# Seven block products for one more pair of batches in a fused attention and two-layer feed-forward kernel, with a new table of order and buffers

## Chip, core and metric

The kernel runs on one core of a Trainium2 chip. The metric is the device time of one execution in microseconds. The core has five engines with a queue of instructions each: TensorE (PE) multiplies matrices into the eight banks of its accumulation memory, VectorE (DVE), ScalarE (ACT) and GpSimd (POOL) do elementwise work, and SyncE (SP) issues the transfers between main memory and on-chip memory. GpSimd works here on on-chip tiles alone, never on a bank.

## The reference, cut to what matters

```python
def _attn_ref(x, state):                      # x 4 x 8 x 512 x 64, state 4 x 8 x 32 x 64
    scores = scale * np.matmul(x, state.transpose(0, 1, 3, 2))
    ...
    xread = np.matmul(softmax(scores), state)
    scores2 = scale * np.matmul(state, x.transpose(0, 1, 3, 2))
    ...
    sread = np.matmul(softmax(scores2), x)
    return np.concatenate([xread, sread], axis=2)

def _moe_ref(x, w_in, w_out):                 # first layer, 2176 tokens, 512 -> 2048 -> 512
    h = x @ w_in
    g = np.maximum(h, 0.0) + np.log1p(np.exp(-np.abs(h)))
    return g @ w_out

def _moe2_ref(x, w_gate, w_val, w_out):       # second layer, 512 -> 1536 -> 512
    g = x @ w_gate
    silu = g * (1.0 / (1.0 + np.exp(-g)))
    return silu * (x @ w_val) @ w_out
```

The attention's result is the input of the first layer, and that layer's result the input of the second.

## The kernel before

Every operand of a large product is split into a high part, rounded to the type fp32r, and a low part, the remainder. A product then is three matmuls: high by high, weight-low by high, weight-high by low (`THREE`).

The first layer's 2048 hidden columns are worked in four chunks `c` of 512, each chunk in four blocks `ft` of 128 columns, and the tokens in four batches `b` of 512. A unit is (c, b, ft) and has the number n = 16c + 4b + ft. The step `p<n>` (function `p1`, L758) makes the unit's hidden block in a bank from the attention weights and the product of state and input weights: six matmuls of 512 columns. `sp<n>` (class `Softplus`) takes the softplus on ScalarE, and `gl<n>` (`g_low`) the low part. The steps `mm`, `mh`, `ml` make the products of state and input weights (L710) and split them; `s1`, `s1h`, `s1l`, `s3`, `s4` carry the 128 state rows through the same layer.

The product with `w_out` goes two ways. For a pair (c, q) of batches 2q, 2q+1 that is not in the set `SEVEN`, each unit has a step `P<n>` (`p2`, L782): its hidden block by the four column blocks of `w_out` into four banks, 12 matmuls, summed over `ft`. After four of them `y_add` moves the banks to the tile `y`. For a pair in `SEVEN`, the two batches and the two halves of `ft` are a 2 by 2 matrix of blocks B11, B12 (batch 2q+1, first half), B21 (batch 2q, second half), B22, and the product with the 2 by 2 matrix of `w_out` is made with seven block products instead of eight: `y_part` (L896) in the order P1, P2, P5, P3, P6, P7, P4, as steps `P<16c+8q>` and on. Each has 12 matmuls in two banks. They need sums of blocks, T1 = B12 - B11, T3 = B22 - B12, T2 = T3 + B11, T4 = B21 - T2 (`g_sum`, L865, steps `g.T1<c><q><f>`), split again (`gh`, L870; `gL`, L877), and sums of the weights (`ws.<c><i>`, L833; `wsh`, L837; `wsl`, L841). P1, P6, P7 and P4 share a pair of banks, and so do P2, P5 and P3; behind each step two additions (`ya`, `yb`, function `y_put`, L796 to L800) bring the banks to `y`.

The second layer (`q1` to `q7`, L1011; `om` L1048; `op` L1072) follows the same scheme, with weights that were split early, stored to main memory and loaded again (`lg<n>`, `lw<n>`, `ls<q>`).

The order of all work is a table of names written out by hand or by a planner, `ORDER`: the kernel calls the steps in that order, each engine executes its instructions in it, and an exclamation mark behind a name moves an elementwise step from its usual engine to the other of VectorE and GpSimd. A second table, `HOMES`, says which bank or buffer holds each tile. Steps `warm` are small matmuls of constants that fill TensorE's time at the start; there are 39 in both kernels.

```python
    SEVEN = {(1, 0), (1, 1), (2, 0), (2, 1), (3, 0), (3, 1)}
    SEQUENCE = ("P1", "P2", "P5", "P3", "P6", "P7", "P4", None)
```

## Time and profile before

| | us |
|---|---|
| median of 3 runs | 711.68 (711.34 to 711.95) |
| the profiled execution | 711.46 |
| its span, first to last record | 709.7 |
| TensorE busy | 701.7 |
| VectorE busy | 567.0 |
| ScalarE busy | 400.7 |
| GpSimd busy | 160.5 |

The span is what the trace covers; the execution's own time has some 1.8 us around it. Busy times count overlapping records of one engine once. The records of matmuls overlap, since one begins before the end of the one ahead.

### The profile page before, as it was taken

How to read it: one execution, taken by the hardware profiler on the slowest of the kernel's cores; microseconds unless marked ns; L12 is line 12 of the kernel's file. 1: busy time of each engine (PE TensorE's matmuls, PEld its weight loads, DVE VectorE, ACT ScalarE, POOL GpSimd, SP SyncE). 2: the span in 40 equal slices, each digit the busy share in tenths (PEclk: the TensorE clock that was granted, in tenths of full speed). 3: DMA queues.
4: the chain of work that ended last, by engine and by line, in shares of the span. 5: the costliest groups of instructions: out<-in, count | busy, mean ns of one | idle time of the engine just before them, and what ended most of it. 6: DMA issues, size and time to landing. Idle time of an engine off the chain costs nothing.

```text
span 709.7 us, 10357 instructions
## 1 busy us (share of the span) xinstructions
PE 701.7 (99%) x3696; PEld 563.8 (79%) x3696; DVE 567.0 (80%) x967; ACT 400.7 (56%) x740; POOL 160.5 (23%) x149
## 2 busy tenths in 40 slices
PE   8999999999999999999999999999999999999997
PEld 5687878786877778888888888888888888887886
DVE  4986545799999999899677788778886988777686
ACT  4987566666775766558665647645552434334231
POOL 0343223325342404250302110013050000122000
PEclk9999999999999999999999999999999999999999
DMA  8980002044142420465867387565969899777603
GB/s 329 397 327 1 1 1 89 31 167 160 54 126 89 149 90 2 142 229 160 271 219 253 121 297 261 184 240 188 357 237 327 299 297 335 265 283 260 249 0 120
DMA packets 48628, 134.90 MB, mean 190 GB/s; under 512 B 5440, under 2 KB 17728, under 8 KB 48576
## 3 DMA queue, kind: packets, MB, share of 16 engines
q1 hardware_dynamic: 48576, 134.24, 53.1%
q8 instruction: 29, 0.48, 0.3%
q14 instruction: 23, 0.19, 0.1%
HBM read 93.06 MB, written 41.16 MB: 189 GB/s over the span
## 4 chain that ended last, share of the span: by engine, by line
PE 97%; DVE 2%; POOL 1%; ACT 0%; issue 0%; ACTq 0%; DVEq 0%
PE b L1011 32%; PE b L896 16%; PE b L758 12%; PE b L1048 11%; PE b L1072 7%; PE b L782 6%; PE b L1096 2%; PE b L710 2%; PE b L954 2%; PE b L974 2%; PE b L1334 1%; PE b L1129 1%; PE b L601 1%; POOL d L833 0%; PE b L681 0%; POOL d L766 0%
## 5 line engine op out<-in xcount | busy, mean ns | idle before, releaser
L1011 PE MATMUL b<-k,k 128*128 128x512 f32 x1008 | 242.6, 390 | 0.0
L1011 PEld LDWEIGHTS b<-k,k 128*128 128x128 f32 x1008 | 187.9, 188 | 39.9 <-ACT d L1270 0.5
L896 PE MATMUL b<-d,k 128*128 128x512 f32 x366 | 98.0, 393 | 0.2
L758 PE MATMUL b<-k,k 128*128 128x512 f32 x384 | 94.9, 392 | 0.0
L1253 DVE TENSOR_TENSOR d<-b,d 128x512 f32<-128x512 f32 x96 | 64.7, 685 | 31.5 <-PE b L1011 23.7
L1270 ACT ACTIVATE d<-b 128x512 f32<-128x512 f32 x72 | 42.5, 592 | 82.9 <-PE b L1011 69.8
L758 PEld LDWEIGHTS b<-k,k 128*128 128x128 f32 x384 | 71.3, 188 | 19.6 <-issue 3.4
L1036 DVE TENSOR_TENSOR k<-b,k 128x512 f32<-128x512 f32 x110 | 73.5, 684 | 16.4 <-PE b L1072 9.1
L896 PEld LDWEIGHTS b<-d,k 128*128 128x128 f32 x366 | 67.7, 188 | 20.0 <-issue 1.0
L1048 PE MATMUL b<-d,k 128*128 128x512 f32 x308 | 77.8, 390 | 0.0
L1048 PEld LDWEIGHTS b<-d,k 128*128 128x128 f32 x308 | 57.5, 188 | 11.8
L800 DVE TENSOR_TENSOR k<-b,k 128x512 f32<-128x512 f32 x84 | 56.4, 684 | 9.6 <-PE b L896 9.2
L421 DVE SCALAR_TENSOR_TENSOR d<-d,k 128x512 int32<-128x512 int32 x65 | 44.8, 696 | 11.9 <-ACT k L415 11.9
L1072 PE MATMUL b<-d,k 128*128 128x512 f32 x202 | 51.7, 391 | 0.0
L1017 ACT ACTIVATE d<-d 128x512 fp32r<-128x512 f32 x58 | 35.4, 626 | 27.0 <-DVE d L1253 11.5
L415 ACT ACTIVATE k<-k 128x512 int32<-128x512 uint32 x68 | 44.9, 669 | 0.0
L1072 PEld LDWEIGHTS b<-d,k 128*128 128x128 f32 x202 | 37.7, 188 | 8.4 <-DVE d L1024 0.5
L766 POOL TENSOR_TENSOR d<-d,d 128x512 fp32r<-128x512 f32 x22 | 30.0, 1367 | 63.3 <-ACT d L745 46.3
L1024 DVE TENSOR_TENSOR d<-d,d 128x512 fp32r<-128x512 f32 x48 | 35.0, 735 | 9.4 <-ACT d L1017 8.3
L896 PE MATMUL b<-k,k 128*128 128x512 f32 x138 | 42.2, 393 | 0.0
L782 PE MATMUL b<-d,k 128*128 128x512 f32 x160 | 39.7, 391 | 0.0
L740 ACT ACTIVATE d<-b 128x512 fp32r<-128x512 f32 x40 | 23.8, 596 | 23.7 <-PE b L758 13.4
(193 smaller groups left out, 1064.4 us busy)
## 6 DMA issues: line engine op xcount, KB each, us to landing
k<-gv_d SPq DMA_DIRECT2D x60, 512.0 KB, 6.9
gv_d<-k SPq DMA_DIRECT2D x48, 512.0 KB, 4.1
k<-in_moe_w_out_dram SPq DMA_DIRECT2D x28, 512.0 KB, 5.6
k<-w_d SPq DMA_DIRECT2D x23, 512.0 KB, 8.1
k<-in_moe_w_in_dram SPq DMA_DIRECT2D x16, 512.0 KB, 7.8
k<-in_moe_w_gate_dram SPq DMA_DIRECT2D x48, 128.0 KB, 3.8
k<-in_moe_w_val_dram SPq DMA_DIRECT2D x48, 128.0 KB, 3.6
w_d<-k SPq DMA_DIRECT2D x12, 512.0 KB, 4.2
```

What stands on the lines that cost most here:

```text
L415: nc.scalar.activation(self.bot, low_word, AF.Copy, bias=-0.5 + 7.5 * 2.0 ** -18, scale=2.0 ** -29 * (1 - 2.0 ** -18),)
L421: nc.vector.scalar_tensor_tensor(out=ti, in0=ti, scalar=3, in1=self.bot, op0=ALU.logical_shift_left, op1=ALU.bitwise_or,)
L758: nc.tensor.matmul(ps, halves[s3], others[t3], start=par == 0 and n3 == 0, stop=par == NPAR - 1 and n3 == 2)
L782: nc.tensor.matmul(yps[c, b, dt], halves[s3], t[t3], start=ft == 0 and n3 == 0, stop=ft == FT - 1 and n3 == 2)
L800: nc.vector.tensor_tensor(out=v, in0=ps, in1=v, op=ALU.add)
L896: nc.tensor.matmul(ps, halves[s3], g[t3], start=part in OPENS and f == 0 and n3 == 0, stop=f == 1 and n3 == 2, skip_group_check=True)
L1011: nc.tensor.matmul(ps, halves[s3], others[t3], start=first and i == 0 and n3 == 0, stop=i == 1 and n3 == 2, skip_group_check=True)
L1036: nc.vector.tensor_tensor(out=v, in0=ps, in1=v, op=ALU.add)
L1048: nc.tensor.matmul(ps, halves[s3], act[n + f, j][t3], start=f == 0 and n3 == 0, stop=f == 1 and n3 == 2)
L1072: nc.tensor.matmul(ps, halves[s3], act[n, t][t3], start=opens and n3 == 0, stop=n3 == 2, skip_group_check=True)
L1253: eng.tensor_tensor(out=o(), in0=x(), in1=y(), op=op)
L1270: op(f"{name}.{n}", lambda n=n, k=k: nc.scalar.activation(fresh(n, k), cs[n]["x"], AF.Copy))
```

## The change

The pair (0, 1), batches 2 and 3 of the first chunk, is made with seven block products. `ORDER` and `HOMES` are rewritten as a whole: the order of every engine changes. In the class that makes the weight sums of the second layer's output, a branch is added for groups q with 2q in `SEVEN2` = {12, 14, 16, 18, 20}; the groups that the kernel makes have q from 0 to 5.

```diff
-    SEVEN = {(1, 0), (1, 1), (2, 0), (2, 1), (3, 0), (3, 1)}
+    SEVEN = {(0, 1), (1, 0), (1, 1), (2, 0), (2, 1), (3, 0), (3, 1)}
...
+            self.now = 2 * q in SEVEN2
...
+                if self.now:
+                    self.raw.append(w2[2 * q + f])
+                    continue
...
+            if self.now:
+                w2s[self.q, k] = o
```

Of the table, the lines around the step P10 after the change, with the one around P10 before, and the lines with the load `lg18` in both:

```diff
-    "al7! hd.w11 p12 hd.w12 s1l.0 hd.w13 P10 tl.w11 tl.o12 tl.w12 p13 P11 sp13 ya11 tl.w13 yb11 sp12 mm.11 ab.o13",
+    "tl.o12 P9 sp12 g.T1011 s1l.0 yb8 hd.w12 gh.T1011 g.T1010 tl.w12 p14 gh.T1010 yb9 gL.T1010! mm.11 sp14",
+    "gL.T1011! ya9 P10 mh.111 g.T3010 ab.o11 ml.111 g.T2010 gh.T3010 g.T4010 gh.T2010 mm.10 ab.o13 gL.T2010! mh.110",
...
-    "op.14P2 lg18 oa.12P40 c1.16 as.16 oa.14P10 th.14B22 oa.12P41 q4.16 th.14T1 os.h31 tL.14T1! op.14P5 oa.14P20",
+    "op.14P5 os.l31! tL.14T2! q6.17 lg18 b2.16 bs.16 op.14P6 th.16B11 b1.17 q5.17 tL.14T3! oa.14P50 q7.17 oa.14P51",
```

TensorE's queue late in the second pair of the first chunk, before: the step P14 (L782, four banks, a weight block d and the hidden block k) and the first-layer step p16 (L758).

```order
L782 MATMUL b_74<-d_882,k_408 128x512 x2
L782 MATMUL b_74<-d_654,k_408 128x512
L782 MATMUL b_75<-d_882,k_408 128x512 x2
L782 MATMUL b_75<-d_654,k_408 128x512
L782 MATMUL b_70<-d_882,k_408 128x512 x2
L782 MATMUL b_70<-d_654,k_408 128x512
L782 MATMUL b_69<-d_882,k_408 128x512 x2
L782 MATMUL b_69<-d_654,k_408 128x512
L758 MATMUL b_72<-k_470,k_818 128x512 x3
L758 MATMUL b_72<-k_390,k_1020 128x512 x3
```

TensorE's queue at the same place after the change, where the lines are numbered 13 higher: two first-layer steps, p19 and p17 (L771), and P13 (L909), a block step on T3 in two banks.

```order
L771 MATMUL b_69<-k_470,k_1036 128x512 x3
L771 MATMUL b_69<-k_394,k_465 128x512 x3
L771 MATMUL b_75<-k_470,k_1036 128x512 x3
L771 MATMUL b_75<-k_394,k_465 128x512 x3
L909 MATMUL b_70<-d_582,k_706 128x512 x2
L909 MATMUL b_70<-d_559,k_706 128x512
L909 MATMUL b_70<-d_1080,k_580 128x512 x2
L909 MATMUL b_70<-k_1083,k_580 128x512
L909 MATMUL b_73<-d_582,k_706 128x512 x2
L909 MATMUL b_73<-d_559,k_706 128x512
L909 MATMUL b_73<-d_1080,k_580 128x512 x2
L909 MATMUL b_73<-k_1083,k_580 128x512
```

A step of 12 matmuls stays one of 12, in two banks instead of four; there is one such step fewer in the pair, and its operands are weights and block sums.

VectorE's queue between the low parts of the state rows (L965) of the first and the second chunk, before: 12 instructions, pieces of weights (L421, L428), low parts of products with the state (L718) and copies to y (L798).

```order
L421 SCALAR_TENSOR_TENSOR d_356<-d_356,k_117 128x512
L428 SCALAR_TENSOR_TENSOR d_220<-k_107,d_220 128x512
L428 SCALAR_TENSOR_TENSOR d_299<-k_105,d_299 128x512
L428 SCALAR_TENSOR_TENSOR d_256<-k_115,d_256 128x512
L798 COPY k_107<-b_73 128x512
L428 SCALAR_TENSOR_TENSOR d_356<-k_117,d_356 128x512
L718 TENSOR_TENSOR k_997<-b_76,k_997 128x512
L798 COPY k_117<-b_75 128x512
```

VectorE's queue between the same two instructions (L978) after the change, a part of the 44 that stand there: the sums of the second block row (L878), their low parts (L890), a low part from a bank (L777) and a copy and an addition to y (L811, L813).

```order
L878 TENSOR_TENSOR d_245<-b_74,d_245 128x512
L878 TENSOR_TENSOR d_141<-d_245,d_141 128x512
L878 TENSOR_TENSOR d_182<-d_182,d_141 128x512
L890 TENSOR_TENSOR k_1066<-d_141,k_826 128x512
L890 TENSOR_TENSOR k_1083<-d_245,d_1080 128x512
L890 TENSOR_TENSOR k_1088<-d_182,d_1085 128x512
L777 TENSOR_TENSOR d_1096<-b_74,d_1057 128x512
L731 TENSOR_TENSOR k_465<-b_76,k_465 128x512
L811 COPY k_576<-b_75 128x512
L428 SCALAR_TENSOR_TENSOR d_314<-d_314,k_109 128x512
L813 TENSOR_TENSOR k_576<-b_70,k_576 128x512
```

The sums and low parts of the new pair stand in one row on VectorE between work on weights that was there before.

## Rows read from the trace of the kernel before

**Rows 1.** Page, busy us (share of the span) and instructions of each engine.

```profile
PE 701.7 (99%) x3696; PEld 563.8 (79%) x3696; DVE 567.0 (80%) x967; ACT 400.7 (56%) x740; POOL 160.5 (23%) x149
```

**Rows 2.** Page, the chain that ended last, share of each engine.

```profile
PE 97%; DVE 2%; POOL 1%; ACT 0%; issue 0%; ACTq 0%; DVEq 0%
```

**Rows 3.** Waits of TensorE: releaser, us in total, times, longest.

```profile
PE b L669 <- ACT d L614: 2.2, 3, 1.1
PE b L1334 <- DVE ones L372: 1.1, 1, 1.1
PE b L1334 <- ACT d L614: 0.4, 1, 0.4
PE b L1334 <- DVE k L718: 0.2, 1, 0.2
```

**Rows 4.** Stretches: length, busy PE, PEld, DVE, ACT, POOL, then granted clock, transfers.

```profile
0.00:17.70 17.70, 14.99 (x106) 9.85 (x106) 8.04 (x20) 7.94 (x16) 1.75 (x7) 1.00 0.88 328
17.70:35.50 17.80, 16.59 (x315) 10.67 (x312) 17.32 (x38) 16.86 (x39) 6.88 (x6) 1.00 1.02 398
35.50:86.20 50.70, 50.70 (x314) 41.33 (x313) 34.27 (x59) 38.14 (x70) 18.38 (x13) 1.00 0.29 115
86.20:122.10 35.90, 35.90 (x208) 27.70 (x207) 19.75 (x33) 21.48 (x41) 10.31 (x10) 1.00 0.14 45
122.10:333.40 211.30, 211.09 (x1066) 165.86 (x1065) 192.11 (x318) 143.27 (x262) 67.81 (x61) 1.00 0.33 111
333.40:692.00 358.60, 358.60 (x1639) 297.33 (x1638) 283.39 (x486) 170.61 (x311) 55.31 (x53) 1.00 0.70 248
```

**Rows 5.** Timeline 59 to 104 us, in parts: start, us covered, instructions merged.

```profile
59.65 0.39 PE L782 MATMUL b<-d,k 128*128 128x512 f32 x1
...
86.62 1.89 DVE L428 SCALAR_TENSOR_TENSOR d<-k,d 128x512 int32<-128x512 int32 x3
90.28 2.88 PE L782 MATMUL b<-d,k 128*128 128x512 f32 x12
...
93.09 1.09 PE L710 MATMUL b<-d,d 64*32 64x512 f32 x16
...
97.29 1.09 ACT L714 ACTIVATE k<-b 128x512 fp32r<-128x512 f32 x2
...
98.21 3.73 PE L954 MATMUL b<-d,d 128*128 128x128 f32 x32
```

**Rows 6.** Groups by line and shape: busy us, mean ns, idle before.

```profile
L865 DVE TENSOR_TENSOR d<-b,d 128x512 f32<-128x512 f32 x20 | 13.5, 684 | 1.7 <-ACT d L745 0.8 <-ACT b L742 0.5 <-POOL k L437 0.3
L833 DVE TENSOR_TENSOR d<-d,d 128x256 f32<-128x256 f32 x7 | 2.9, 420 | 0.1
L877 POOL TENSOR_TENSOR d<-d,k 128x512 fp32r<-128x512 f32 x3 | 3.9, 1300 | 30.2 <-PE b L896 21.8 <-ACT k L870 8.4
L870 ACT ACTIVATE d<-d 128x512 fp32r<-128x512 f32 x32 | 19.7, 626 | 20.6 <-PE b L896 12.8 <-DVE d L865 5.6 <-POOL d L865 1.3
L742 ACT ACTIVATE b<-b 128x512 f32<-128x512 f32 x24 | 14.3, 596 | 2.3 <-PE b L758 2.2
```

**Rows 7.** Timeline 122 to 140 us, first pair of the second chunk.

```profile
122.08 3.30 PE L896 MATMUL b<-d,k 128*128 128x512 f32 x12
122.83 2.14 PEld L896 LDWEIGHTS b<-d,k 128*128 128x128 f32 x10 [0.55 <-POOL d L766]
...
136.14 1.42 PE L896 MATMUL b<-d,k 128*128 128x512 f32 x5
...
139.38 0.84 PE L974 MATMUL b<-k,k 128*128 128x512 f32 x3
```

**Rows 8.** Loads of the second layer's split gate and value weights (L520), issue to landing.

```profile
DMA to landing us min/median/max: 3.9/6.9/11.4
```

**Rows 9.** Timeline at P0 and at the last addition.

```profile
41.33 2.91 PE L782 MATMUL b<-d,k 128*128 128x512 f32 x12
...
705.83 0.69 DVE L1036 TENSOR_TENSOR k<-b,k 128x512 f32<-128x512 f32 x1 [0.67 <-PE b L1048]
```

540 rows, old and new, of tables (HOMES, ORDER) are left out of this document.

## Prediction

> **What bounds the kernel now.** First I read the page's busy times: TensorE (PE) is busy 99% of the span (709.7 us), VectorE (DVE) 80% and ScalarE (ACT) less [rows 1]. The chain of work that ended last then says whether that share is the path: 97% of it is TensorE's [rows 2]. Third, the list of waits on TensorE names everything that it waited for: 3.9 us in all, and each releaser belongs to the first layer's attention or to the start (L614 is the exponential of the scores, L372 the first constant) [rows 3]. Fourth, busy times by stretch: TensorE lacks 2.7 us of the first 17.7 us and 1.2 us of the next 17.8, and from then on only 0.2 us until 692 us [rows 4]. So behind the start the reader is to see one engine that never stands still for long: a matmul taken out there shortens the run by its own pitch, if the work in front of the next matmul is ready.
>
> A busy TensorE can hide short waits, since its records overlap. So I also looked at the pitch: twelve second-layer matmuls of the first chunk (L782) that follow each other cover 2.88 us, one record alone 0.39, so eleven steps take 2.49 us, or 0.226 us each [rows 5]. Such blocks are the ones that the change touches, and they run without a pause. The granted clock is 1.00 throughout, the level of 2.4 GHz [rows 4].
>
> **What the change removes.** In the first chunk, batches 2 and 3 have eight steps P8 to P15 of 12 matmuls of 512 columns each. After the change there are seven, P8 to P14, of 12 each (two banks, two blocks, three products). No other group of matmuls changes in number; the filler matmuls are the same 39. So 12 x 0.226 = **2.72 us** leave TensorE, in a stretch where it is 100% busy.
>
> The Trainium skill ("TensorE: Matmul & The Clock Gate", "Back-to-back issue gap") gives about 131 ns as the sustained pitch of such matmuls with weight loads between them. By it twelve would be worth an estimated 1.57 us. This trace has 0.226 us for this very line, and the measurement decides, so I give the page's figure no chance.
>
> **What it adds.** By the table and the functions: 8 block sums (L865), 8 roundings (L870), 8 low parts (L877), 2 weight sums of four half-width instructions (L833) with 4 roundings and 4 low parts, and 6 more additions into the y tile (L800), while 2 low parts of the first layer fall away. As the lists of instructions count it, VectorE gets 16 more, GpSimd 16, ScalarE 12. One costs 0.68 us on VectorE (0.42 half wide), 1.30 on GpSimd, 0.63 on ScalarE [rows 6]. All of this would be some 10 us of VectorE, put at nothing on the path because TensorE runs meanwhile: from P8 to P16 VectorE was busy 19.75 of 35.90 us [rows 4].
>
> Is that cover enough? In the table from P8 to P16 I count 38 full-width and 4 half-width VectorE instructions before, 57 and 8 after. In line, three full-width ones take 1.89 us, so the pitch is (1.89 - 0.69) / 2 = 0.60 us [rows 5]. Then 57 x 0.60 + 8 x 0.42 = 37.6 us. TensorE has there seven block steps of 2.72, ten first-layer steps of 6 x 0.226 = 1.36, three score products of about 1.25 (1.09 for the row and its start), and one state product of 3.7 us [rows 5]: 19.0 + 13.6 + 3.75 + 3.7 = 40.1 us. So 2.5 us of VectorE stay free; without the overlap of neighbours (0.684 each [rows 6]) it would need 39.0 + 3.4 = 42.4 us, 2.3 too many. Which applies? From 122 to 333 us VectorE ran 318 instructions in 211.3 us and TensorE lacked 0.2 us [rows 4]; that stretch keeps its number of VectorE instructions in the table to within 16 short ones. I take the pitch.
>
> **Hand-offs in the new pair.** A block step can't start before its operand is summed, rounded and has its low part. The tightest that I find is P10, on T1 = B12 - B11. Behind p12 TensorE has P9, p14 and one score product, 2.72 + 1.36 + 1.25 = 5.3 us. VectorE has nine instructions from T1's first sum to its last low part, 5.4 us by the pitch, and may begin some 0.6 us before p12 ends, because p13, 1.36 us earlier, feeds the first (a softplus of 0.60 lies between): it ends at 4.9, 0.4 us ahead. Such margins can fail. The same hand-off exists in the first pair of the next chunk: there the first block step took 3.30 us for its twelve instead of 2.88, a loss of 0.42, its weight loads having waited for GpSimd's low part [rows 7]; the step P18 took 139.38 - 136.14 = 3.24 us to the next group instead of 2.72, a loss of 0.52. So the new pair costs between 0 and 0.94 us more; I take the one of the opening step, **0.42 us**, as its margins are of the size of these losses.
>
> **The order of the rest.** All other instructions are reordered. Up to P0 both tables have the same TensorE steps, and the waits there come to 2.8 us apart from the first constant [rows 3]: that much could go at most. Ahead of P0, which starts at 41.3 us [rows 9], stand one more full VectorE step and two more ScalarE steps in the table, 0.60 + 2 x 0.49 = 1.6 us if nothing hides them (two ScalarE instructions in line cover 1.09 us [rows 5], one about 0.60). I put the start at no change, ends -2.8 and +1.6. The tail keeps its shape: VectorE's last addition starts at 705.83 us and a store follows [rows 9].
>
> **Sum.** The profiled execution took 711.46 us: its span of 709.7 and 1.8 around it. 711.46 - 2.72 + 0.42 = **709.2 us**. The median of the runs, 711.68, stands 0.2 above the profiled one, which I leave inside the range.
>
> **The rivals.**
> The start gets longer (0.10): attention's exponentials already hold TensorE up there, and more steps now stand in front; against it, TensorE needs nothing of these extra steps before P0. 711.46 - 2.72 + 1.6 = 710.3 us; 710.8 with the hand-off.
>
> VectorE becomes the bound from P8 to P16 (0.12): for it, 0.684 us is what one instruction occupies, and the stretch goes from half full to nearly full; against it, the pitch of neighbours is 0.60, and fuller stretches passed without a wait. 711.46 - 2.72 + 2.3 = 711.0 us: the gain is nearly eaten. The Trainium skill ("Perfetto Trace Analysis", "Identifying the Most-Contended Engine") takes occupancy as the fair measure for Vector and not for matmuls; weight loads at 79% would stand level with VectorE's 80% here, and by that rule it is this rival that comes true.
>
> A late weight load makes it slower (0.06): the place is the load lg18 ahead of the step q1.18 in the second half. Before, 11 TensorE steps of 1.36 us stand between them in the table, 15.0 us; after, four (op.14P6, q5.17, q7.17, op.14P3), 5.4 us. Loads of this kind land after 3.9 to 11.4 us, 6.9 in the median [rows 8]. SyncE's queue issues in order, so later loads move with it. At the median the wait is 1.5 us, time 710.7; at the longest 6.0 us, time 709.2 + 6.0 = 715.2. From a landing of 9.4 us it is slower by over 0.2%. Against it: TensorE waited for no such load before [rows 3], leads of 6.8 us (lg13, lg16) among them, and the first product needs only the first of four tiles.
>
> The start gets shorter (0.05): its longest single wait of 1.1 us goes [rows 3], 711.46 - 2.72 - 1.1 = 707.6 us. The edit in the weight sums of the second half changes nothing: its condition asks for 2q among 12 to 20, and q goes to 5.
>
> **How the numbers follow.** The likeliest case, TensorE shorter by its twelve matmuls and hand-offs of 0 to 0.94 us, holds 0.67: 708.7 to 709.7, forecast 709.2. 0.2% of 711.46 is 1.42 us, about what a measurement of this kernel can tell from no change; so faster is below 710.0, slower above 712.9. Faster: 0.67 and 0.05, and of the start-up and VectorE cases, which need not reach their full price, 0.07: 0.79. Slower: the late load from 9.4 us on, 0.04. The rest, 0.17, is the same. The range for 8 in 10 reaches from the shorter start, 707.6, to the VectorE bound, 711.0; it leaves out the longer loads and, at the low end, a start without any wait.
>
> **What the profile after would show.** TensorE 12 matmuls fewer (3684), busy 2 to 3 us less, its busy time still 99%, and no wait over 0.3 us by the list behind 40 us: then the first term is right. In the new pair, block steps that cover over 2.9 us show the hand-off's price; two of them at 0.4 or more put the sum too low. VectorE over 95% busy in the stretch around P8 to P16 with TensorE's weight loads waiting for VectorE would be the second rival; a wait of TensorE on a load of gv_d behind 500 us the third. The prediction is wrong if P0 starts more than 1 us from its place before, 41.3 us, or if the stretch behind P16 loses more than it did.

## Result and the profile after

The changed kernel takes 716.29 us in the median (715.55 to 716.44, 4 runs) against 711.51 of the kernel before (711.32 to 711.95, 4 runs): ratio 1.0064, 95% interval 1.0047 to 1.0082. It is slower by 4.8 us where 2.3 us less were forecast. Executions of one kernel with and without a fall of TensorE's clock (below) stand together in a median. Lines below carry the changed kernel's numbers: 7 above those of before up to L531 (before's L421 is L428, its L428 is L435, its L437 is L444), 13 above from L583 on.

The page of the profiled execution (716.37 us, span 714.6), busy us by engine, to be held against [rows 1]: TensorE has its 12 matmuls fewer and is busy 1.0 us *longer*.

```profile
PE 702.7 (98%) x3684; PEld 561.2 (79%) x3684; DVE 584.0 (82%) x983; ACT 408.4 (57%) x752; POOL 178.7 (25%) x165
```

Waits of TensorE after (releaser, us in total, times, longest), beside [rows 3]. The longest one on the exponential (L627, before's L614) has grown from 1.1 to 1.9 us, and four kinds of 0.5 us and more are new: L795 on GpSimd, L707 on ScalarE, L771 on VectorE, L1024 on a transfer.

```profile
PE b L682 <- ACT d L627: 2.8, 2, 1.9
PE b L1347 <- DVE ones L379: 1.0, 1, 1.0
PE b L795 <- POOL d L779: 0.9, 1, 0.9
PE b L707 <- ACT d L703: 0.9, 2, 0.4
PE b L771 <- DVE d L777: 0.8, 1, 0.8
PE b L1024 <- DMA k<-gv_d: 0.5, 2, 0.3
```

To see where the time went, both spans are cut at the same steps: P0, P8, P16 (stretch, length, busy PE, PEld, DVE, ACT, POOL, granted clock, transfers). First before, at 41.33, 79.27 and 122.08:

```profile
0.00:41.33 41.33, 37.41 (x503) 25.39 (x504) 29.86 (x65) 30.27 (x65) 11.11 (x15) 1.00 0.96 369
41.33:79.27 37.94, 37.94 (x196) 30.74 (x195) 25.36 (x43) 28.67 (x53) 13.47 (x11) 1.00 0.24 91
79.27:122.08 42.81, 42.81 (x239) 33.41 (x238) 24.14 (x40) 25.47 (x48) 12.72 (x12) 1.00 0.12 38
122.08:709.70 587.62, 583.50 (x2763) 474.29 (x2761) 487.68 (x822) 316.32 (x576) 123.14 (x114) 1.00 0.55 195
```

The same of the changed kernel:

```profile
0.00:43.90 43.90, 38.10 (x503) 25.34 (x504) 31.00 (x66) 30.64 (x65) 11.90 (x16) 0.96 0.89 334
43.90:83.45 39.55, 38.63 (x196) 30.58 (x195) 33.01 (x55) 30.37 (x57) 14.83 (x12) 1.00 0.19 76
83.45:124.76 41.31, 40.51 (x228) 30.93 (x227) 35.33 (x60) 28.87 (x53) 6.14 (x5) 1.00 0.14 39
124.76:714.60 589.84, 585.49 (x2763) 474.37 (x2761) 484.64 (x805) 318.55 (x579) 145.84 (x134) 1.00 0.56 196
```

TensorE's counts agree in every stretch but the pair's (3696 and 3684 in all). The start is 2.57 us longer, P0 to P8 1.61 longer, the changed pair 1.50 *shorter*, the rest 2.22 longer: +4.90 in all. So the place that the edit names did gain, though 1.2 us less than its matmuls, and three places that the forecast put at no change lost 6.4.

What TensorE and its releasers do at those places, from the timeline after (start, us covered, engine, line, instructions merged, the idle time before):

```profile
10.74 0.63 PE L682 MATMUL b<-ident,d 128*128 128x128 f32 x4 [1.92 <-ACT d L627]
...
12.03 1.96 PE L614 MATMUL b<-k,d 64*32 64x512 f32 x16
...
25.58 1.36 POOL L664 TENSOR_TENSOR d<-d,r 128x512 f32<-128x512 f32 x1 [6.51 <-DVE r L660]
25.96 0.67 DVE L643 TENSOR_REDUCE m<-d 128x16 f32<-128x512 f32 x1
...
27.91 1.04 POOL L664 TENSOR_TENSOR d<-d,r 128x512 f32<-128x512 f32 x1
28.00 1.50 DVE L428 SCALAR_TENSOR_TENSOR d<-d,k 128x512 int32<-128x512 int32 x1 [0.32 <-ACT k L422]
28.60 2.04 PE L723 MATMUL b<-d,d 64*32 64x512 f32 x16
...
48.29 1.88 PE L795 MATMUL b<-d,k 128*128 128x512 f32 x7 [0.92 <-POOL d L779]
...
97.72 0.69 DVE L890 TENSOR_TENSOR d<-d,d 128x512 fp32r<-128x512 f32 x1 [0.60 <-ACT d L883]
98.33 0.68 DVE L777 TENSOR_TENSOR d<-b,d 128x512 fp32r<-128x512 f32 x1
99.07 1.66 PE L771 MATMUL b<-k,k 128*128 128x512 f32 x6 [0.80 <-DVE d L777]
...
134.37 1.58 PE L723 MATMUL b<-d,d 64*32 64x512 f32 x16
...
616.21 6.14 SPq L583 DMA_DIRECT2D k<-w2s_d  x2
622.47 1.98 SPq L527 DMA_DIRECT2D k<-gv_d  x4
629.03 0.94 PE L1024 MATMUL b<-k,k 128*128 128x512 f32 x3 [0.21 <-DMA k<-gv_d]
```

Four readings. TensorE stands 1.92 us ahead of the first transposes (L682), and a score product behind them (L614) takes 1.96 us for its sixteen matmuls where before it took 1.09. A product of state and weights at 28.60 takes 2.04 us against 1.09 [rows 5]: one of its weight blocks comes from L428, which lasts 1.50 us there. At 99.07 the first-layer step p15 waits until VectorE has read its bank (L777); that step of VectorE stands behind a low part (L890) which waited 0.60 us for ScalarE's rounding (L883). At 629 a product waits for a load (L527, lg20) that stood in SyncE's queue behind a load of weight sums (L583), which itself waited 6 us for a buffer.

The granted clock belongs to the first reading. The stretches after: at 11.37, behind the idle time, it drops to 0.50 (1.2 GHz) for 3.4 us.

```profile
0.00:11.37 11.37, 8.18 (x54) 6.28 (x55) 2.67 (x7) 2.06 (x3) 0.70 (x6) 1.00 0.81 276
11.37:14.79 3.42, 3.42 (x24) 1.53 (x24) 1.63 (x4) 2.34 (x5) 1.05 (x1) 0.50 1.03 418
```

### The profile page after: what moved, and what is told of

Its sections match the earlier page's. It is cut to its first block, busy times and chain, and to the rows that moved or that the text cites. A ratio compares the mean times of both kernels' runs of the same rounds, so it can differ in the third digit from the quotient of the medians.

```text
span 714.6 us, 10385 instructions
## 1 busy us (share of the span) xinstructions
PE 702.7 (98%) x3684; PEld 561.2 (79%) x3684; DVE 584.0 (82%) x983; ACT 408.4 (57%) x752; POOL 178.7 (25%) x165
## 4 chain that ended last, share of the span: by engine, by line
PE 92%; DVE 3%; DMA 3%; POOL 1%; issue 1%; ACT 1%; SPq 0%; ACTq 0%; POOLq 0%
PE b L1024 30%; PE b L909 19%; PE b L771 13%; PE b L1061 11%; PE b L1085 6%; PE b L795 3%; PE b L1109 2%; PE b L723 2%; PE b L967 2%; PE b L987 2%; PE b L1142 1%; DMA k<-gv_d 1%; DMA k<-in_xt_dram 1%; DMA w2s_d<-k 1%; PE b L1347 1%
## 5 line engine op out<-in xcount | busy, mean ns | idle before, releaser
L1024 PE MATMUL b<-k,k 128*128 128x512 f32 x1008 | 243.5, 391 | 0.5 <-DMA k<-gv_d 0.5
L1024 PEld LDWEIGHTS b<-k,k 128*128 128x128 f32 x1008 | 187.6, 188 | 40.4 <-DVE k L1049 0.8
L909 PE MATMUL b<-d,k 128*128 128x512 f32 x576 | 141.1, 394 | 0.0
L909 PEld LDWEIGHTS b<-d,k 128*128 128x128 f32 x576 | 106.4, 188 | 30.8 <-issue 2.5
L771 PE MATMUL b<-k,k 128*128 128x512 f32 x384 | 94.7, 393 | 0.8 <-DVE d L777 0.8
L1049 DVE TENSOR_TENSOR k<-b,k 128x512 f32<-128x512 f32 x110 | 73.0, 685 | 21.3 <-PE b L1085 12.7
L771 PEld LDWEIGHTS b<-k,k 128*128 128x128 f32 x384 | 71.2, 188 | 20.7 <-DVE d L777 1.7
L1061 PE MATMUL b<-d,k 128*128 128x512 f32 x336 | 82.8, 390 | 0.0
L779 POOL TENSOR_TENSOR d<-d,d 128x512 fp32r<-128x512 f32 x35 | 48.9, 1410 | 113.7 <-ACT d L758 54.1
L1061 PEld LDWEIGHTS b<-d,k 128*128 128x128 f32 x336 | 63.0, 188 | 13.6 <-DVE d L1037 0.3
L1030 ACT ACTIVATE d<-d 128x512 fp32r<-128x512 f32 x63 | 38.9, 627 | 43.8 <-DVE d L1266 25.2
L813 DVE TENSOR_TENSOR k<-b,k 128x512 f32<-128x512 f32 x90 | 60.5, 684 | 3.6 <-PE b L909 3.0
L428 DVE SCALAR_TENSOR_TENSOR d<-d,k 128x512 int32<-128x512 int32 x67 | 48.9, 739 | 10.1 <-ACT k L422 9.9
L1085 PE MATMUL b<-d,k 128*128 128x512 f32 x210 | 53.3, 392 | 0.0
L883 ACT ACTIVATE d<-d 128x512 fp32r<-128x512 f32 x54 | 33.2, 627 | 29.3 <-PE b L909 20.1
L1085 PEld LDWEIGHTS b<-d,k 128*128 128x128 f32 x210 | 39.0, 188 | 9.2 <-DVE k L1049 0.9
L1037 DVE TENSOR_TENSOR d<-d,d 128x512 fp32r<-128x512 f32 x52 | 36.6, 714 | 8.9 <-PE b L1085 4.7
L441 ACT ACTIVATE k<-d 128x512 fp32r<-128x512 f32 x52 | 32.3, 626 | 19.1 <-PE b L1024 8.3
L753 ACT ACTIVATE d<-b 128x512 fp32r<-128x512 f32 x50 | 29.7, 593 | 16.3 <-PE b L909 8.5
```

The source lines that it names most:

```text
L428: nc.vector.scalar_tensor_tensor(out=ti, in0=ti, scalar=3, in1=self.bot, op0=ALU.logical_shift_left, op1=ALU.bitwise_or,)
L771: nc.tensor.matmul(ps, halves[s3], others[t3], start=par == 0 and n3 == 0, stop=par == NPAR - 1 and n3 == 2)
L779: eng.tensor_tensor(out=l, in0=sp[u].g, in1=sp[u].h.bitcast(F32), op=ALU.subtract)
L813: nc.vector.tensor_tensor(out=v, in0=ps, in1=v, op=ALU.add)
L909: nc.tensor.matmul(ps, halves[s3], g[t3], start=part in OPENS and f == 0 and n3 == 0, stop=f == 1 and n3 == 2, skip_group_check=True)
L1024: nc.tensor.matmul(ps, halves[s3], others[t3], start=first and i == 0 and n3 == 0, stop=i == 1 and n3 == 2, skip_group_check=True)
```

## Experiments

My theory after the result: the twelve matmuls are worth their price, and the loss is a handful of waits that the rewritten table makes elsewhere. The rival: the seven block products themselves, with their sums and low parts, cost more than they save. Each run below is of the changed kernel with one edit, if nothing else is said; the median of before beside these runs was 711.55 to 711.83 us.

**e1, fillers.** Four filler steps are moved, two from ahead of the first score product and two from behind the first transposes, so that they stand between that score product and these transposes, three of the four just ahead of the transposes.

```diff
-    ... x30 warm.1.pa0_1 warm.1.sc2_1 warm.1.sc0_1 warm.1.pa0_0
-    sc0 x31 sc1 mx0 nm0 mx1 ld.w01 e0 ts1 pa0 nm1 warm.1.sc2_0 M1 a0 warm.1.pa2_1 sc5
+    ... x30 warm.1.sc0_1 warm.1.pa0_0
+    sc0 x31 warm.1.pa0_1 sc1 mx0 nm0 mx1 warm.1.sc2_1 warm.1.sc2_0 warm.1.pa2_1 ld.w01 e0 ts1 pa0 nm1 M1 a0 sc5
```

> Kernel after with four of its filler matmuls moved from ahead of sc0 and behind pa0 to between sc0 and pa0, as the kernel before has one there; none is added. Theory 1 (the clock): TensorE stood still for 1.92 us before pa0, the granted clock then fell to 0.5 from 11.4 to 14.8 us, and the two score products in that stretch took 1.96 us instead of 1.09, fillers and transposes there some 0.5 more. With the gap filled the clock stays at 1.0, sc5 ends about 1.4 us earlier, the first block step P0 starts at 42.2 to 43.0 us instead of 43.9, and the time is 714.6 to 715.4 us (716.3 less 0.9 to 1.7). Theory 2 (the order of the rest of the start holds P0: ScalarE's and VectorE's steps): the clock may stay at 1.0, but P0 remains within 0.4 us of 43.9 and the time at 716.3.

714.29 us (714.15 to 715.42, 5 runs), ratio 1.0041 (1.0029 to 1.0053). Its timeline has fillers (L1347) where the idle time was, the score product L614 takes 1.09 again, and the clock is 1.00 throughout:

```profile
10.07 0.94 PE L1347 MATMUL b<-ones 128*128 128x128 f32 x6
10.84 0.60 PE L682 MATMUL b<-ident,d 128*128 128x128 f32 x4
11.37 1.09 PE L614 MATMUL b<-k,d 64*32 64x512 f32 x16
```

P0 comes at 42.50 instead of 43.90, and all that gain is kept: theory 1 holds. It is the fall that costs, and hardly the wait: e5 below has no filler moved, the same wait of 1.92 us and no fall, and its P0 comes at 42.63 (in e7 at 42.41 and in e3 at 43.01, with the same wait and no fall).

```profile
10.88 0.63 PE L682 MATMUL b<-ident,d 128*128 128x128 f32 x4 [1.92 <-ACT d L627]
...
11.89 1.09 PE L614 MATMUL b<-k,d 64*32 64x512 f32 x16
```

Without the fall the kernel is still 2.7 us slower than before.

**e2, a buffer.** Ahead of 48.29 us P1 waits 0.92 us for the low part l0_0_1, which must wait until P0 has read l0_0_0 from the same buffer. It gets another.

```diff
-    "l0_0_0 l0_0_1 h0_0_3 ...
+    "l0_0_0 h0_0_3 ...
-    "l0_0_3 l0_1_2 ...
+    "l0_0_1 l0_0_3 l0_1_2 ...
```

> Kernel after with one name moved in the table of buffers: the low part l0_0_1 leaves the buffer of l0_0_0, which P0 reads, and gets a free one. Theory 1 (the buffer): TensorE's wait of 0.9 us on the low part L779 in P1, and about 1.1 us of lost time with it, is that buffer; GpSimd then starts this low part some 1.5 us earlier, the wait is gone, the time is 716.3 - 1.1 = 715.2 us. Theory 2 (GpSimd or the softplus before it is late anyway): the wait stays over 0.5 us and the time at 716.3.

715.03 us (713.11 to 717.03, 6 runs), ratio 1.0048 (1.0034 to 1.0063). P1 runs without a gap; a small wait appears behind it:

```profile
46.60 2.99 PE L795 MATMUL b<-d,k 128*128 128x512 f32 x12
...
50.26 5.28 PE L771 MATMUL b<-k,k 128*128 128x512 f32 x22 [0.21 <-DVE k L677]
```

P0 to P2 falls from 12.23 to 11.53 us. The wait is real, and 0.7 of its 0.9 us come back; the total scatters too widely to show it.

**e3, a bank.** p15 takes the bank of p12 and goes ahead of mm.10, a product of state and input weights, so that it needn't wait for L777. The second half of mm.10 gets the bank that L777 reads.

```diff
-    ... gh.T2010 mm.10 ab.o13 gL.T2010! mh.110 gl14 wh.o12 ml.110 p15 mh.100
+    ... gh.T2010 p15 ab.o13 gL.T2010! mh.110 gl14 wh.o12 ml.110 mm.10 mh.100
```

> Kernel after with p15 writing the bank of p12 instead of that of p14, and placed ahead of mm.10, which takes over p14's bank for its second half. Theory 1 (the bank): the wait of 0.8 us before p15 at 99 us, on the low part gl14 that still reads p14's bank, goes; TensorE loses 0.1 to 0.3 us there instead of 0.9; 716.3 - 0.8 = 715.5 us. Theory 2 (VectorE is full there and something else of its queue becomes the wait): the stretch 95 to 125 us keeps its length to 0.2 us, with another releaser named, and the time stays at 716.3.

714.61 us (713.94 to 716.37, 5 runs), ratio 1.0047 (1.0035 to 1.0059). The wait is gone from the list, but P8 to P16 only goes from 41.31 to 41.18 us, since the product (L723) now waits inside itself:

```profile
96.17 1.52 PE L771 MATMUL b<-k,k 128*128 128x512 f32 x6
97.62 1.60 PE L723 MATMUL b<-d,d 64*32 64x512 f32 x16
```

Theory 2 by its number, since the stretch keeps its length to 0.13 us: the wait moves to the next user of that bank. What makes L777 late is its place in VectorE's queue more than a lack of time there: in this profile too VectorE stands idle for 0.60 us, waiting for L883, just ahead of L890 and L777. This execution also had the same 1.92 us of idle time in the start, and no fall of the clock: its first product there took 1.09 us.

**e4, a load.** The prediction's third rival: lg18 goes ahead of the load ls1, thirteen TensorE steps ahead of q1.18 (four in the changed kernel, eleven in the kernel before).

```diff
-    q6.17 lg18 b2.16 ... op.12P4 b1.16 ls1
+    q6.17 b2.16 ... op.12P4 lg18 b1.16 ls1
```

> Kernel after with the weight load lg18 put ahead of the load ls1 in SyncE's queue; ls1 stood in the queue for 6 us there, waiting for its buffer. Theory 1: lg18 is issued some 6 us earlier, TensorE's wait on gv_d at 629 to 630.5 us (0.5 us by the list of waits, 0.8 to 1.0 us of lost time) goes; 716.3 - 0.9 = 715.4 us. Theory 2 (lg18 then waits for its own buffers, or ls1 becomes late for op.14P5): the loss moves to another place, the time stays at 716.3 or above.

720.78 us (717.03 to 723.15, 6 runs), ratio 1.0122 (1.0100 to 1.0144). The list of waits shows why: the load of weight sums behind lg18 now comes late.

```profile
PE b L1085 <- DMA k<-w2s_d: 3.3, 1, 3.3
```

The clock falls to 0.50 for another 3.4 us behind that wait. lg18 wasn't late in the changed kernel at all; the load that TensorE waits for at 629 us is lg20.

**e5, the buffer ahead of lg20.** The weight sum w2s2_1, whose load held SyncE's queue for 6 us, gets a buffer that is free earlier.

```diff
-    "w2o3_0 w2s2_1 gw21_1_1",
+    "w2o3_0 gw21_1_1",
-    ... oacc1_0 w2s4_1",
+    ... oacc1_0 w2s2_1 w2s4_1",
```

> Kernel after with one name moved in the table of buffers: w2s2_1, the second half of the load ls2, takes a buffer that has been free since the first half of the second layer, instead of the one from which a store to w2s_d had still to land. By the order of TensorE's steps the wait on gv_d at 629 us stands in q2.20, so the late load is lg20 (and not lg18): in SyncE's queue it stands behind ls2, which held the queue from 616.2 to 622.4 us. Theory 1: ls2 no longer holds the queue, lg20 is issued 1 to 2 us earlier (its second tile still waits for op.16P1, which ends at 620.5), the wait on gv_d (0.5 us in the profile of after, 0.8 in another execution of the same steps) falls under 0.1 and TensorE's lost time from 620 to 640 us from 1.1 to 0.3 us; 716.3 - 0.8 = 715.5 us. Theory 2 (the transfers themselves are slow there): lg20 lands at the same time, the wait stays.

715.08 us (714.17 to 715.89, 5 runs), ratio 1.0050 (1.0037 to 1.0063). The load holds the queue for 1.18 us now. No wait on gv_d is in its profile, but e1 had none either without this edit: the price of that load differs between executions, and I count it at 0 to 0.8 us (0.8 in the profile of e2).

**e6, the late weight block.** e1, and the block that L428 makes at 28.00 us is made earlier; one other tile (e23_1) gets another buffer for that.

```diff
-    ... hd.w01 e6 warm.1.pr2_1 pa7 hd.w00 sr4 pa6 a3 r0 pr5 a2 hd.w03
-    ... warm.1.pm0_0_0 ab.w02 warm.1.pr1_1 warm.1.pm0_2_0 mi3 tu1 pr3 bt.w02 so2 hd.w02 ti0 a6
+    ... hd.w01 e6 ab.w02 warm.1.pr2_1 pa7 hd.w00 sr4 pa6 bt.w02 a3 r0 pr5 a2 hd.w03 hd.w02
+    ... warm.1.pm0_0_0 warm.1.pr1_1 warm.1.pm0_2_0 mi3 tu1 pr3 so2 ti0 a6
```

> Kernel e1_fillers with the preparation of the weight piece w02 (two ScalarE steps, one VectorE step) put back to where the kernel before has it, ahead of the readings of batches 2 and 3, and e23_1 in another buffer so that w02's can be written then. Theory 1: in after and in e1_fillers the first product of batch 0 with the weights, mm.00, took 2.04 us instead of 1.09 since its third block of rows waited for w02's VectorE step, which took 1.5 us instead of 0.65 beside GpSimd's work; with it early mm.00 takes 1.09 us and P0 starts 0.9 us earlier than in e1_fillers, at 41.6 us, within 0.3 us of the kernel before; 714.3 - 0.9 = 713.4 us. Theory 2 (ScalarE bounds the start): the two ScalarE steps moved ahead delay what followed them, P0 stays at 42.5 us within 0.3 and the time at 714.3.

717.37 us (715.36 to 719.00, 6 runs), ratio 1.0079 (1.0064 to 1.0094). The block is early now (L428 at 25.32, 0.69 us long), but its ScalarE work stands in front of the attention's:

```profile
PE b L707 <- ACT d L703: 2.3, 2, 2.1
```

The clock falls to 0.50 from 28.11 to 31.53 us, so the product at 28.99 still takes 1.96 us, and P0 comes at 44.24. Theory 2: in the start ScalarE has no room for this work earlier.

**e7, a further step less.** P14 issues none of its 12 matmuls.

```diff
-            for f in range(2):
+            for f in range(0 if (c, q, part) == (0, 1, "P4") else 2):
```

> Kernel after without the twelve matmuls of the last block step P14 of the new pair; everything else, its additions into y too, is kept, so the y of batches 2 and 3 lacks this block product. Theory 1 (a matmul taken out of the new pair is worth its pitch, TensorE is the bound there): P8 to P16 takes 41.3 - 2.7 = 38.6 us, and the time is 716.3 - 2.7 = 713.6 us. Theory 2 (VectorE, nearly full there, bounds the pair, so the twelve matmuls that the change took out were worth little): P8 to P16 stays within 0.7 us of 41.3, with new waits of TensorE on VectorE, and the time at 715.6 or more.

716.15 us (715.40 to 718.68, 6 runs), ratio 1.0069 (1.0057 to 1.0082): a second twelve give nothing, and P8 to P16 takes 42.49 us instead of 41.31. The timeline has the place, behind which the clock falls (its start had the wait of 1.92 us and no fall, with P0 at 42.41):

```profile
114.81 1.66 PE L771 MATMUL b<-k,k 128*128 128x512 f32 x6
118.58 5.97 PE L771 MATMUL b<-k,k 128*128 128x512 f32 x18 [2.12 <-DVE k L811]
```

TensorE waits for a bank that VectorE hasn't copied yet; VectorE's steps follow each other with no idle time of 0.2 us or more from 112.45 us to the end of that copy. So in the changed kernel VectorE is next behind TensorE in this stretch.

**e8, all at once.** e6, e2, e3 (with mm.10 behind s1.1 and mh.100 behind it), e5, and mm.13 put behind p23.

```diff
-    gl14 wh.o12 ml.110 p15 mh.100 gL.T3010! gh.T4010 ml.100 s1.1 sp15 ya10
+    gl14 wh.o12 ml.110 gL.T3010! gh.T4010 s1.1 mm.10 sp15 mh.100 ya10 ml.100
```

> Kernel after with all that was found undone together: fillers and w02 as in e6_w02, the free buffer of e2_buffer, p15 in p12's bank with mm.10 behind s1.1, the free buffer of e5_gate, and mm.13 one step later, behind p23 (its second half waited there for an addition that reads its bank). Theory 1 (the change's twelve matmuls are worth 2.7 us, and the table of buffers and the order took back 7 to 8): time lost by TensorE falls from 26.2 to about 21 us; 716.3 - 1.4 - 0.9 - 0.7 - 0.9 - 0.8 - 0.5 = 711.1 us, between 710.0 and 712.0, about that of the kernel before; P0 at 41.6 us, P8 to P16 in 40.5 us. Theory 2 (the waits only move, as one more step is late behind each): P16 starts at 123.5 us or later and the time is above 713.

720.79 us (719.41 to 721.86, 4 runs), ratio 1.0127 (1.0114 to 1.0140). Each wait taken away has a successor:

```profile
PE b L707 <- ACT d L703: 2.5, 2, 2.2
PE b L909 <- ACT k L883: 2.5, 1, 2.5
PE b L967 <- DVE k L731: 1.1, 1, 1.1
```

The second is of my own making. The low part of the product that I moved back (ml.100, L731) still stands ahead of the block sums (L878) in VectorE's queue:

```profile
105.17 0.69 DVE L731 TENSOR_TENSOR k<-b,k 128x512 fp32r<-128x512 f32 x1 [4.38 <-ACT k L727]
```

The first sum behind it starts at 105.77 instead of 101.88 us, and the rounding L883 waits for the sums.

**e9, the twelve put back.** e1, and P10 issues its 12 matmuls twice, with nothing else changed.

```diff
-            for f in range(2):
+            for f in (0, 1, 0, 1) if (c, q, part) == (0, 1, "P5") else (0, 1):
```

> Kernel e1_fillers in which the block step P10 of the new pair, which opens its banks, issues its twelve matmuls twice (the second time starts the banks anew, so the result is the same): as many matmuls in the new pair as the kernel before has there, all else as after. Theory 1 (what the change took out was worth its pitch): P8 to P16 goes from 41.3 to 44.0 us and the time from 714.3 to 717.0 us. Theory 2 (VectorE's queue bounds the new pair, so the twelve were worth little): the wait of 0.8 us before p15 and others on VectorE shrink by what is added, P8 to P16 grows by under 1 us, and the time stays under 715.3. In between, with the wait before p15 alone swallowed: 2.7 - 0.9 = 1.8 us, 716.1 us.

718.23 us (717.39 to 719.89, 4 runs), ratio 1.0095 (1.0081 to 1.0109). P8 to P16 goes from 41.25 us in e1 to 44.02, by 2.77; the forecast's 12 x 0.226 are 2.72. The median rises by 3.94, 1.2 us more: in the profile the way from P16 to the last matmul is 1.50 us longer than in e1, which the twelve don't explain. For TensorE this refutes the rival: the matmuls taken out save what they should. What the sums, roundings and low parts of the new pair cost elsewhere it doesn't show, as both versions have them.

**e10, the start once more.** e6 with the steps st2 and so2 behind the product mm.00.

```diff
-    ... n10 st2 warm.1.pm0_0_0 ... pr3 so2 ti0 a6 warm.1.pm0_1_0 mm.00 M2
+    ... n10 warm.1.pm0_0_0 ... pr3 ti0 a6 warm.1.pm0_1_0 mm.00 st2 so2 M2
```

> Kernel e6_w02 with the state's transpose st2 of batch 2 and its ScalarE step moved behind mm.00, where the kernel before has it; in e6_w02 TensorE waited 2.1 us before st2 for a ScalarE step that w02's had pushed back. Theory 1 (order of the start alone): st2 waits no more, mm.00 takes 1.09 instead of 2.04 us, and P0 starts at 41.6 us (e1_fillers 42.5); 714.3 - 0.9 = 713.4 us. Theory 2 (ScalarE bounds the start, so what is gained at mm.00 is lost at the next step that needs ScalarE): P0 stays at 42.3 us or later, the time at 714.1 or above.

718.04 us (715.77 to 719.54, 5 runs), ratio 1.0086 (1.0072 to 1.0101). P0 at 45.21: the wait moves to `PE b L1347 <- ACT d L686`, 1.9 us in two pieces, and the clock falls behind the longer one. Theory 2 again.

**e11, three together.** e1, e2, e5, and mm.13 behind p23 (from 134.37 us, where its second half waited for a bank).

```diff
-    ... gh.T1100 mm.13 ab.w20 gL.T1100! sp22 tl.e0.0 p23 yb17
+    ... gh.T1100 ab.w20 gL.T1100! sp22 tl.e0.0 p23 mm.13 yb17
```

> Kernel e1_fillers with the free buffer of e2_buffer, the free buffer of e5_gate, and mm.13 one step later, behind p23 (its second half waited for an addition that reads its bank, 1.58 instead of 1.09 us). Theory 1 (these losses are separate): 714.3 - 0.7 (P1) - 0.5 (mm.13) - 0 to 0.6 (q2.20, which waited in some executions) = 712.5 to 713.1 us; P16 at 122.5 us. Theory 2 (each wait only moves to the next late step): 714.0 or above.

713.54 us (713.35 to 713.86, 8 runs), ratio 1.0027 (1.0016 to 1.0037): above what I expected (712.5 to 713.1). P0 to P2 is 12.12 us, not e2's 11.53, because a step ahead of P1 now waits for ScalarE (L707 on L703, 0.28 us).

**e12, before with the gap.** The kernel *before*, with four of its start's fillers out and one moved, so that TensorE stands 1.92 us ahead of the first transposes there too.

```diff
-    x00 warm.12.sc0_0 ... warm.1.pa2_1 sc0 x31 warm.1.pa0_1 mx0 sc1
+    x00 warm.8.sc0_0 ... warm.1.pa2_1 warm.1.pa0_1 sc0 x31 mx0 sc1
```

> Kernel before with its filler between sc0 and sc1 moved ahead of sc0, as the change has it, and four of the twelve fillers at the very start left out, so that sc0 is not held up by them and TensorE stands still longer before pa0. Theory 1 (the fillers keep the clock): TensorE is idle for 1.5 to 2 us before pa0, the granted clock falls to 0.5 for some 3.4 us in most executions, the next score products take 1.9 us instead of 1.09, and P0 starts 1.0 to 1.6 us later than at 41.3; 712.5 to 713.1 us. Theory 2 (the clock's fall in the changed kernel has another cause than this gap): the clock stays at 1.0 and the time within 0.4 us of 711.55.

711.69 us (711.18 to 712.48, 11 runs), ratio 1.0000 (0.9991 to 1.0009). With the same gap the clock stayed at 1.00 in the profile, and P0 was at 41.65. In 5 of its 11 executions the mean clock was 0.998 or less (median 712.2 us, the other six 711.6), so it may fall there; theory 2, that the gap alone isn't enough, holds for most.

**e13, spliced.** Before's order up to P6, the changed kernel's from P7 to P16, before's behind, with a table of buffers of my own.

```diff
-    SEVEN = {(1, 0), (1, 1), (2, 0), (2, 1), (3, 0), (3, 1)}
+    SEVEN = {(0, 1), (1, 0), (1, 1), (2, 0), (2, 1), (3, 0), (3, 1)}
```

> The seven block products of the new pair in the order of the kernel before: its order of all work up to P6, then the changed kernel's order from there to P16 (the new pair, with some twenty steps moved a few places), then the order of the kernel before again; the table of buffers is made anew for it, each value going to the buffer that has been free longest. Theory 1 (the seven products are worth their twelve matmuls, and what the change lost lies in the rewritten table outside of the new pair): P0 at 41.3 to 41.6 us as in the kernel before, P8 to P16 in 40 to 41.5 us instead of 42.8, no new wait of TensorE over 0.5 us, the time 711.5 - 2.7 + 0 to 1.2 = 708.8 to 710.0 us, faster than the kernel before. Theory 2 (the products themselves cost as much as they save, by VectorE's extra steps and the hand-offs behind P16): P16 no earlier than at 121.5 us, and the time 711.0 us or above.

715.60 us (715.11 to 716.75, 5 runs), ratio 1.0054 (1.0042 to 1.0067). In its profile the clock falls to 0.50 from 10.70 to 14.11 us, behind a wait of only 0.54 us, and P0 comes at 42.54. The waits are many, 1.3 us the longest; P0 to P8 takes 40.46 us and P16 to the last matmul 2.8 us more than before. By the numbers it is theory 2, with P16 at 124.64 us and a time above 711.0. But the buffers were new as well, so it doesn't separate the seven products from the tables.

**e14, spliced, with the twelve.** e13 with e9's edit.

> e13_spliced with the twelve matmuls of P10 issued twice (the second time starts the banks anew): as many matmuls as the kernel before, with all the extra work of the seven products. Theory 1: P8 to P16 is 2.7 us longer than in e13_spliced, and the time by 2.7 us (2.2 to 3.2), that is at 711.5 us or above. Theory 2 (VectorE bounds the new pair there): under 1 us longer.

718.39 us (718.18 to 719.57, 4 runs), ratio 1.0097 (1.0081 to 1.0112). P8 to P16 is 44.30 us against 41.64 in e13: the twelve are worth 2.66 here. And P0 stands at 41.38, as before (41.33): the same start as e13's, without the fall.

**e15, two engines kept apart.** e11, with the GpSimd step that overlaps L428 at 28.00 us moved to VectorE.

```diff
-    ... pr3 bt.w02 so2 hd.w02 ti0 a6
+    ... pr3 bt.w02 so2 hd.w02 ti0! a6
```

> This is the version with three waits taken away (713.54 us), with one step moved from GpSimd to VectorE: the product with the reciprocal of batch 0's item 0 (L664, ti0), which now stands in VectorE's queue directly behind the low half of the third weight block (L428, hd.w02). In the profile of that version L428 begins at 26.61, 0.08 us after a GpSimd step (26.53 to 27.58), and lasts 1.51 us where L428 otherwise takes 0.63 to 0.69; the score product that reads it (L723 x16, from 27.20) takes 2.06 us where such a product takes 1.09. Theory 1, the two engines hold each other up when VectorE's step reads two operands from SBUF: with GpSimd idle there, L428 at 26.6 takes 0.7 us, the product L723 x16 takes 1.1 to 1.4, and all behind it comes 0.6 to 0.9 earlier if nothing else waits next: P0 at 41.7 to 42.0 in place of 42.58, time 712.6 to 713.0. Theory 2, the length of L428 has nothing to do with GpSimd: it takes 1.5 us again, the product 2.0 and the time is 713.5 or, by VectorE's extra 0.7 us, up to 714.2. Theory 3, sharing is real but VectorE's queue is next: L428 takes 0.7 and the product 1.1, and the extra 0.7 us in VectorE's queue makes a later wait of the same size: P0 at 42.4 to 42.8, time 713.3 to 713.8.

713.93 us (712.69 to 714.72, 11 runs), ratio 1.0023 (1.0013 to 1.0032). The timeline of e15: L428 has its usual length, and the product L723 is 0.83 us shorter than in e11 (2.06).

```profile
26.80 0.69 DVE L428 SCALAR_TENSOR_TENSOR d<-d,k 128x512 int32<-128x512 int32 x1 [0.31 <-ACT k L422]
27.42 0.68 DVE L664 TENSOR_TENSOR d<-d,r 128x512 f32<-128x512 f32 x1
...
27.40 1.23 PE L723 MATMUL b<-d,d 64*32 64x512 f32 x16
```

P0 comes at 41.98 against 42.58. That the engines hold each other up (theory 1) is shown; what it is worth in the total is not. The median is no better than e11's and above the forecast (712.6 to 713.0). P8 keeps 0.43 us of the gain (81.74 against 82.17), with a wait for GpSimd's low part L779 of 0.7 us between P2 and P8 that e11 hasn't, and the start of the last matmul none (708.61 against 707.85), and the times lie in two groups, 712.7 to 713.3 and 713.9 to 714.7, of which the profile shows the second.

## Why the prediction was wrong

**The table of stretches against the sum** (us, from the two profiles):

| stretch | before | after | difference | predicted |
|---|---|---|---|---|
| start to P0 | 41.33 | 43.90 | +2.57 | 0 (-2.8 to +1.6) |
| P0 to P8 | 37.94 | 39.55 | +1.61 | 0 |
| P8 to P16 | 42.81 | 41.31 | -1.50 | -2.72 + 0.42 |
| P16 to the span's end | 587.62 | 589.84 | +2.22 | 0 |

**"12 x 0.226 = 2.72 us leave TensorE": right.** Put back they cost 2.77 (e9) and 2.66 us (e14).

**"0.42 us" for hand-offs: mis-sized.** P8 to P16 shortened by 1.50 us instead of the 2.77 of e9, so 1.27 us went to waits, above my upper end of 0.94. I looked for them ahead of block steps, where an operand is summed. The largest, 0.80 us, stands ahead of the first-layer step p15, which waits for VectorE to *empty* a bank; that step of VectorE stood behind another, which waited 0.60 us for ScalarE. e3 gave that bank to another product, and the wait went with it.

**"VectorE becomes the bound": not yet, but next.** Its 60 instructions took 35.33 of 41.31 us; I had 37.6 of 40.1. e7 shows how little was left. I also read the stretch before wrongly: 86.20 us is where P10 starts. P8 starts at 79.27, and from there to P16 VectorE was busy 24.14 of 42.81 us, not 19.75 of 35.90; the sum didn't use this.

**"I put the start at no change": this step failed.** I counted steps and weighed their sum, +1.6 at worst, but didn't ask what a longer wait does to the clock, nor whether two engines would meet. The fall of the clock cost 1.40 us at P0 (e1); the wait behind which it came costs little by itself, as P0 at 42.63, 42.41 and 43.01 in e5, e7 and e3 shows beside 42.50 in e1. The product with the long L428 cost 0.83 more (e15), of which P0 had 0.60. The fall doesn't come in every execution of this start: all four executions of the changed kernel have a mean clock of 0.997 or 0.998, while of the ten of e3 and e5, whose start is the same, seven have 0.999 or more, with a median of 714.3 us, that of e1.

**"The order of the rest" as a term of 0: failed too.** The prediction said that all other instructions were reordered and then priced the start alone. Its own signs of being wrong came: P0 2.57 us late, a stretch behind P16 that lost more, and waits of 0.9 and 0.8 us behind 40 us. It had no term for P0 to P8, where one shared buffer costs 0.7 us (e2), though VectorE has 12 instructions more there as well (55 instead of 43), and none behind P16, where 2.22 us were lost: 0 to 0.8 to lg20, 0.24 to mm.13 (P16 to P24 takes 38.34 us in e11 and 38.58 in e1), the rest in pieces under 0.5 us.

**The late load: right in kind, wrong in place.** I named lg18 and q1.18 by their distance in the table; the load that came late was lg20, which stood behind a load that waited for its buffer (e5). lg20's lead had shrunk too, from eight TensorE steps to five, so distance in the table alone didn't tell which of the two would be late: it says nothing of what stands in SyncE's queue in between, as e4 showed at a price of 4.5 us. By its own terms this rival is slower by 0.2% from a landing of 9.1 us on, not 9.4.

**What stays open.** e1 accounts for 2.0 of the 4.8 us in medians and e11 for 2.75. By the profiles e11's last matmul still starts 2.45 us behind before's: +1.25 at P0, +1.65 to P8, -1.53 in the pair, +1.08 behind. Part of that is the meeting of VectorE and GpSimd (below), but only one meeting was taken away. How much of the 6.4 us is the tables and how much the new pair's own extra work on VectorE, GpSimd and ScalarE isn't shown: every version of the changed order has both. Why the clock falls at 11.37 us in the changed kernel's profile and not in e3, e5, e7 and e12 with the same idle time isn't settled; the last part has what goes with it. No version here beats the kernel before, and e11 is the best of the changed ones.

## What to carry to other kernels

A rewritten table of order needs a term for every stretch that it reorders, not for the one where work is removed: the twelve matmuls were worth 2.7 us as forecast, while the stretches that the edit doesn't name lost 6.4, 1.4 of them to a fall of the clock that most executions of e3 and e5, with the same start, don't have. Before a wait is mended, look at who stands next in the releaser's queue; five of ten repairs here (e3, e4, e6, e8, e10) only moved it, and those that put work earlier into a full queue of ScalarE or SyncE made it worse. Taking the removed work back in (e9) and taking more out (e7) priced the edit and showed the next bound faster than the repairs did.

## What the runs showed of the hardware

**VectorE and GpSimd hold each other up.** In the timeline after, L428 begins 0.09 us into a GpSimd step and takes 1.50 us; without GpSimd it takes 0.69 (e15). The reduction L643, which reads one tile, begins 0.38 us into a GpSimd step and takes 0.67, as it does alone. Nor does a VectorE step get longer that reads one of its operands from a bank: of the 90 additions to y after (L813), the 40 that overlap a GpSimd step have a mean of 682 ns and the longest takes 692, the other 50 have 685. GpSimd is lengthened as well, where VectorE comes first; after, around 51 us:

```profile
46.96 1.27 POOL L779 TENSOR_TENSOR d<-d,d 128x512 fp32r<-128x512 f32 x1 [1.53 <-PE b L707]
50.86 3.51 POOL L779 TENSOR_TENSOR d<-d,d 128x512 fp32r<-128x512 f32 x2 [2.62 <-PE b L795]
...
50.82 0.69 DVE L428 SCALAR_TENSOR_TENSOR d<-d,k 128x512 int32<-128x512 int32 x1
51.55 1.67 DVE L435 SCALAR_TENSOR_TENSOR d<-k,d 128x512 int32<-128x512 int32 x1
```

A step of GpSimd takes 1.27 us at 46.96 and two in line at 50.86 take 3.51; L435 between them takes 1.67. The Trainium skill ("SBUF — State Buffer", "Who interferes with whom") states that a VectorE instruction with two inputs in SBUF, the memory of the tiles, contends with a GpSimd instruction that reads SBUF, and that issue order, not op shape, decides who blocks. These rows agree. Two groups by shape ahead of 320 us have more of it in the changed order. Before:

```profile
L428 DVE SCALAR_TENSOR_TENSOR d<-k,d 128x512 int32<-128x512 int32 x30 | 20.6, 699 | 0.2
L437 DVE TENSOR_TENSOR k<-d,k 128x512 fp32r<-128x512 f32 x21 | 15.8, 752 | 1.7 <-ACT k L434 1.5
```

After, the same two groups (mean ns of one behind the busy time):

```profile
L435 DVE SCALAR_TENSOR_TENSOR d<-k,d 128x512 int32<-128x512 int32 x32 | 25.1, 793 | 0.2
L444 DVE TENSOR_TENSOR k<-d,k 128x512 fp32r<-128x512 f32 x20 | 16.0, 798 | 0.9 <-ACT k L441 0.8
```

The mean of the one goes from 699 to 793 ns, of the other from 752 to 798. Counted over both traces, VectorE has 73 steps of 128x512 before with two operands from tiles that overlap a GpSimd step, and 83 after; 31 and 42 of them take over 0.76 us, which adds 14.7 and 20.8 us to the usual 0.685 each. Of such steps that overlap none, no one does.

**A fall of TensorE's clock behind a wait isn't certain.** Granted 0.50 for 3.4 us, it came with or behind waits of 0.54 (e13), 1.7 (e10), 1.9 (after, e2, e4), 2.1 to 2.2 (e6, e7, e8) and 3.3 us (e4), and didn't behind the same 1.92 us in the starts of e3, e5, e7 and e12, nor behind 2.5 us in e8. In the start it goes with how early the clock rose. The fillers (L1347) show that moment: they follow each other every 0.21 us before it and every 0.11 us after it. It came at 3.87 to 5.12 us in the four profiles with a fall in the first 15 us (after, e2, e4, e13), and at 5.85 us or later in before, e3, e5, e7, e12 and e14, which have such waits in the start without a fall. The moment differs between executions of the same instructions. That it decides is not shown.

**A product's two halves overlap only if both may start.** The sixteen matmuls of 64 rows (L723) take 1.09 us together, hardly more than eight of them (1.06 us for the score products at 9.06 in the timeline before), and 1.58 to 2.04 where the second half waits for an operand or a bank. With mm.13 moved behind p23 (e11), its 1.58 became 1.09.
